# A three-stage attention and feed-forward kernel: order of the first weight loads, place of the later weight conversions, and order of three pools at the join to the last layer

## The chip, the cores and the metric

The kernel runs on one core of one Trainium2 chip. The metric is the time of one execution on the device in microseconds, lower is better. TensorE is called PE in the profile (PEld its weight loads), VectorE DVE, ScalarE ACT, GpSimd POOL, SyncE SP; here SP only issues transfers.

## What is computed

The reference has three parts; each one's output is the next one's input. In the attention, keys and values are first pooled into 32 memory slots per head:

```
a = softmax(phi over the sequence)             # 8 x 8 heads, 576 positions, 32 slots
k_m, v_m = einsum(a, k), einsum(a, v)          # 32 x 64 per head
attn = softmax(q @ k_m.T / 8) @ v_m            # q and k are drawn 200 times larger
x  = attn as (4608, 512)
x1 = (silu(x @ w_gate) * (x @ w_val)) @ w_out  # 512 -> 1536 -> 512, "first layer"
h  = x1 @ w_in                                 # 512 -> 2048, "second layer"
out = where(h > 0, h, exp(min(h, 0)) - 1) @ w2_out   # 2048 -> 512
```

All weights arrive as 64-bit floats. [...]

## The kernel before

**Conversion of a weight tile.** `load_w` (line 87) fetches a 128x512 tile of 64-bit numbers (512 KB) into a buffer of pool `wr` (4 buffers) by a transfer that SP issues (line 89), and then rebuilds it: one ACT instruction (line 101) and four on DVE (lines 102, 103, 105, 106). A gate/value tile (`load_wg`, `split=False`) ends with one more DVE addition (line 113). A tile that is used as a sum of two reduced-precision halves (`load_wo`, `load_w2`) ends with an ACT copy (line 108) and two operations (lines 110, 111), on DVE for the first four output tiles (`own`) and on POOL for all others. Once the first unit has run, line 99 keeps a conversion's instructions behind the last `h` that was computed at the time of its tracing.

**First layer, first pass.** Eight batches of 576 tokens. The value matrix of the attention is folded into the gate and value weights: `vw(b, p)` (line 135) multiplies a batch's pooled values with the tiles `WG[p]`. A unit is then a gate product, a value product, a nonlinearity on ACT and DVE, and a split of the result (`gate1`, `val1`). The first pass runs units 0 to 3 of all batches (weights `WG[0]`, `WG[1]`, output tiles `WO[0]` to `WO[3]`) and, between these units, the attention of the batches to come: `front_tasks(b + 2)` (softmax of phi, pooling of keys and values) and `back_tasks(b + 1)` (scores, their softmax). The list `todo` holds those tasks in the order written; `tick()` takes some of them after every step. The weights `WG[2]`, `WG[3]` and `WO[4]` to `WO[7]`, which only the second pass uses, are converted as items of that list (lines 400 to 409).

**Second pass and third.** The next two passes over the batches (lines 502 to 522) run units 4 to 7 and 8 to 11, adding to partial sums that lie in DRAM; conversions of the remaining weights come from the list `conv`. **Second layer:** nine blocks of 512 tokens with 16 units each (lines 580 to 591): 12 matmuls up, minimum, exponential, tanh, product and maximum on DVE and ACT, a split into two halves, and 12 matmuls down two units later. Ten weight conversions are left over for its first block; `w2q` says from which pool each takes its tiles.

**What sets the order.** The program is written as one stream; a scheduler with a timing model gives each engine its order, with the written order as priority. Each engine works through its own order without overtaking. Pools are taken from two stacks of on-chip memory; a pool that is opened where others were closed overlays their tiles, and its first tiles wait until the old tiles at these addresses are no longer used. At the join to the second layer (lines 526 to 531) the right-hand stack loses `p1` (partial sums), `av` (attention outputs), `t` and `h` (first-layer temporaries and results), and gets `wc` (weights), `h3` (results of a second-layer unit) and `t3` (temporaries of a unit), in this order.

Sizes per partition, from the shapes and buffer counts: `h` 18,432 bytes, then `t` 4,608, `av` 18,432, `p1` 4,608. In their place: `wc` 24,576, `h3` 16,384, `t3` 8,192. So `t3` begins 40,960 bytes in and overlays the end of `av`, all of `p1`, and memory beyond it.

**At the start**, line 361 loads phi and all five key/value tiles of batch 0, then the four gate/value tiles of `WG[0]` and the two query tiles (lines 362 to 367).

Of the kernel before, what the change touches and what calls it, by code (L numbers as in the profile page):

```python
# [27 lines left out]
NCH = 5  # L28
# [9 lines left out]
def attention_moe_moe(ctx: ExitStack, tc: tile.TileContext, qT, phiT, kv, kv4, w1g, w1o, w2, out):  # L38
# [5 lines left out]
    w1g, w1o, w2 = w1g.bitcast(I32), w1o.bitcast(I32), w2.bitcast(I32)  # L44
# [5 lines left out]
    wa_p = ctx.enter_context(tc.tile_pool(name="wa", bufs=NWA))  # L50
# [33 lines left out]
                call()  # L84


    def load_w(store, u, i, src, pool, split=True, own=False):
        raw = wr_p.tile([128, 512, 2], I32, tag="wr", name="wr")
        nc.sync.dma_start(out=raw, in_=src.rearrange("p (n t) -> p n t", t=2))
        lo32, hi32 = raw[:, :, 0], raw[:, :, 1]  # L90
        if split:
            hi = pool.tile([128, 512], F32R, tag="w", name="whi")
            lo = pool.tile([128, 512], F32R, tag="w", name="wlo")
        else:
            full = pool.tile([128, 512], F32, tag="w", name="wg")
        v = wt_p.tile([128, 512], F32, tag="wv", name="wv")
        c = wt_p.tile([128, 512], I32, tag="wc", name="wc")
        vi, cf = v.bitcast(I32), c.bitcast(F32)
        with tc.issue_after(last["h"].ins) if "h" in last else nullcontext():

            act(out=v, in_=hi32.bitcast(F32), func=AF.Copy, scale=2.0 ** -112)
            nc.vector.tensor_scalar(out=c, in0=vi, scalar1=3, scalar2=None, op0=ALU.logical_shift_left)
            stt(out=vi, in0=vi, scalar=-2 ** 31, in1=c, op0=ALU.bitwise_and, op1=ALU.bitwise_or)

            nc.vector.tensor_scalar(out=c, in0=vi, scalar1=-2 ** 23, scalar2=None, op0=ALU.bitwise_and)
            stt(out=cf, in0=lo32.bitcast(U32), scalar=2.0 ** -52, in1=cf, op0=ALU.mult, op1=ALU.mult)
            if split:
                act(out=hi, in_=v, func=AF.Copy)
                part = tt if own else nc.gpsimd.tensor_tensor
                part(out=v, in0=v, in1=hi.bitcast(F32), op=ALU.subtract)  # L110
                part(out=lo, in0=v, in1=cf, op=ALU.add)
            else:
                tt(out=full, in0=v, in1=cf, op=ALU.add)
        store[u][i] = (hi, lo) if split else full


    WG = [[None] * KD for _ in range(NU1 // 2)]
# [1 line left out]
    W2 = [[None] * 2 for _ in range(NU2)]  # L119

    def load_wg(p, k, pool):
        load_w(WG, p, k, w1g[p, k], pool, False)

    def load_wo(u, pool):
        load_w(WO, u, 0, w1o[u], pool, own=u < UA)
# [3 lines left out]


    VW = {}

# [57 lines left out]
    class Batch:  # L192
# [13 lines left out]
        def load_q(self, hf):  # L206
            t = self.qr[hf] = bk_p.tile([128, 4, HS], F32, tag="qr", name="qr", bufs=NQ)
            nc.sync.dma_start(out=t, in_=qT[self.b, hf].rearrange("p (j s) -> p j s", j=4))
# [142 lines left out]
    def load(z):  # L351
        z.load_phi()
        for c in range(NCH):
            z.load_kv(c)
# [3 lines left out]
            z.load_q(c)  # L358


    load(Bs[0])
    Bs[0].phi()
    run(front_tasks(0))
    for k in range(KD):
        load_wg(0, k, wa_p)
    load_q(Bs[0])
    run(back_tasks(0))
    vw(0, 0, G2)
    for k in range(KD):
# [14 lines left out]
    def load2(b):  # L384
        at2[b] = av_p.tile([128, 2, 2, S], F32R, tag="at", name="at2")
        nc.sync.dma_start(out=at2[b].bitcast(F32), in_=at_d[b].bitcast(F32))
# [3 lines left out]
    for b in range(B):  # L390
# [3 lines left out]
        if b == 0:  # L394
            wo = [lambda u=u: load_wo(u, wa_p) for u in range(UA)]
            f1 = [lambda: (Bs[1].phi(), load_q(Bs[1]))] + list(front_tasks(1)) + [lambda: Bs[2].phi()]
            for i in range(max(len(wo), len(f1))):
                todo += wo[i:i + 1] + f1[i:i + 1]
        if 1 <= b <= 4:
            bk += [lambda k=k, p=2 + (b - 1) // 2: load_wg(p, k, wa_p) for k in (0, 1) if b % 2] + \  # L400
                [lambda k=k, p=2 + (b - 1) // 2: load_wg(p, k, wa_p) for k in (2, 3) if b % 2 == 0]
        if b == B - 2:
            wb_p = ctx.enter_context(tc.tile_pool(name="wb", bufs=NWB))
            ps_vw = ctx.enter_context(tc.tile_pool(name="ps_vw", bufs=1, space=PSUM))
            V2 = [(ps_vw, "vw"), (ps_gv, "g")]
            fr += [lambda u=u: load_wo(u, wb_p) for u in (4, 5, 6)]
        if b == B - 1:
            fr.append(lambda: load2(0))
            fr += [lambda: load_wo(7, wb_p), lambda: vw(0, 2, V2), lambda: vw(0, 3, V2)]
        for i in range(max(len(bk), len(fr))):  # L410
            todo += fr[i:i + 1] + bk[i:i + 1]
        if b + 1 < B:
# [112 lines left out]
    pend = []  # L525
    st_p1.close()
    st_r.close()
    wc_p = ctx.enter_context(tc.tile_pool(name="wc", bufs=NWC, side="right"))
    w2q = [wa_p] * 4 + [wc_p] * 6
    h3_p = ctx.enter_context(tc.tile_pool(name="h3", bufs=4, side="right"))  # L530
    t3_p = ctx.enter_context(tc.tile_pool(name="t3", bufs=2, side="right"))


    NC3 = T // 128
# [45 lines left out]
    for j in range(NB):  # L580
        xt, accs = nxt, []
        for u in range(NU2):
            pend.append((j, u, unit3(u, xt), accs))
            if len(pend) > LAG:
                down3(pend.pop(0))
            if w2q:
                more_w2(w2q.pop(0))
            if u == NU2 // 2 and j + 1 < NB:
                nxt = load3(j + 1)
# [38 lines left out]
```

## Time and profile before

| | us |
|---|---|
| three runs: lowest, median, highest | 1585.65, 1587.75, 1588.77 |
| the profiled execution's own time | 1587.06 |
| its span from first to last instruction | 1584.9 |
| PE busy | 1523.7 (96% of the span) |
| DVE busy | 1013.3 (64%) |
| ACT busy | 649.6 (41%) |
| POOL busy | 113.4 (7%) |

A span of the profile is 2.2 us shorter than that execution's own time. "Granted clock" is the share of TensorE's full clock (2.4 GHz) that it was given: 1.00 is full, 0.50 is 1.2 GHz. In an instruction's row, the bracket at the end gives how long the engine stood idle before it and what ended this.

### The profile page before, as it was taken

The numbers are of one execution on the slowest core, as the hardware profiler recorded it, in microseconds if no ns is written. First come the engines' busy times: TensorE is split into PE (matmuls) and PEld (weight loads), VectorE is DVE, ScalarE is ACT, GpSimd is POOL, SyncE is SP. The second block draws the span as 40 slices with busy tenths as digits, with TensorE's granted clock in tenths as the row PEclk, the third lists the DMA queues.
The fourth block names the chain that finished last, engine by engine and source line by source line (L and its number), as shares of the span: only waits on it lengthen the run. The fifth ranks groups of instructions, "written<-read, shape, count | busy, mean of one in ns | idle before, by whom it ended". The sixth has DMA issues, their size and how long they took to land.

```text
span 1584.9 us, 24325 instructions
## 1 busy us (share of the span) xinstructions
PE 1523.7 (96%) x9816; PEld 1307.8 (83%) x9816; DVE 1013.3 (64%) x1798; ACT 649.6 (41%) x1249; POOL 113.4 (7%) x87
## 2 busy tenths in 40 slices
PE   4699999999999999999989999999999999999998
PEld 2567889899999999899967888888888888888887
DVE  7999777635666666667798655555555555555554
ACT  3555544533333333433444434333343434343332
POOL 0000000200011112111343000000000000000000
PEclk7899999999999999999999999999999999999999
DMA  9788422425444455544520101010010101010000
GB/s 361 247 298 310 154 95 73 165 77 190 160 158 167 157 175 180 190 157 154 171 72 9 54 1 54 0 47 8 2 52 1 54 1 53 1 54 0 27 1 27
DMA packets 81008, 164.63 MB, mean 104 GB/s; under 512 B 7168, under 2 KB 54272, under 8 KB 77824
## 3 DMA queue, kind: packets, MB, share of 16 engines
q1 hardware_dynamic: 71680, 153.64, 28.4%
q10 hardware_dynamic: 9216, 9.44, 1.7%
q8 instruction: 77, 1.26, 0.3%
q14 instruction: 35, 0.29, 0.1%
HBM read 115.87 MB, written 47.19 MB: 103 GB/s over the span
## 4 chain that ended last, share of the span: by engine, by line
PE 84%; DVE 11%; DMA 3%; issue 1%; ACT 1%; SPq 0%; ACTq 0%; DVEq 0%
PE acc L567 8%; PE acc L568 8%; PE acc L569 8%; PE pu L543 8%; PE pu L541 8%; PE pu L542 8%; PE acc L158 4%; PE acc L160 4%; PE acc L159 4%; PE pg L153 3%; PE pv L153 3%; PE pg L155 3%; PE pv L155 3%; PE pv L154 3%; PE pg L154 3%; PE pvw L141 3%
## 5 line engine op out<-in xcount | busy, mean ns | idle before, releaser
L541 PE MATMUL pu<-x1s,whi 128*128 128x512 f32 x576 | 225.2, 391 | 4.9 <-DVE g L557 4.9
L567 PE MATMUL acc<-whi,hh 128*128 128x512 f32 x576 | 224.4, 390 | 1.4 <-ACT hh L164 1.4
L543 PE MATMUL pu<-x1s,wlo 128*128 128x512 f32 x576 | 225.1, 391 | 0.0
L542 PE MATMUL pu<-x1s,whi 128*128 128x512 f32 x576 | 225.1, 391 | 0.0
L569 PE MATMUL acc<-whi,hl 128*128 128x512 f32 x576 | 222.5, 390 | 2.6 <-DVE hl L166 2.6
L568 PE MATMUL acc<-wlo,hh 128*128 128x512 f32 x576 | 224.1, 389 | 0.0
L556 DVE SCALAR_TENSOR_TENSOR g<-e,g 128x512 f32<-128x512 f32 x144 | 105.7, 735 | 161.4 <-ACT g L555 161.4
L164 ACT ACTIVATE hh<-g 128x512 fp32r<-128x512 f32 x144 | 91.0, 632 | 216.1 <-DVE g L557 213.1
L554 ACT ACTIVATE e<-g 128x512 f32<-128x512 f32 x144 | 90.7, 631 | 214.9 <-DVE g L553 214.8
L185 DVE SCALAR_TENSOR_TENSOR h<-s,pv 128x288 f32<-128x288 f32 x192 | 86.4, 450 | 110.8 <-PE pv L155 93.5
L166 DVE TENSOR_TENSOR hl<-g,hh 128x512 fp32r<-128x512 f32 x144 | 99.5, 691 | 90.0 <-ACT hh L164 89.9
L158 PE MATMUL acc<-hh,whi 128*128 128x288 f32 x512 | 151.2, 298 | 0.0
L159 PE MATMUL acc<-hh,wlo 128*128 128x288 f32 x512 | 150.0, 294 | 0.0
L160 PE MATMUL acc<-hl,whi 128*128 128x288 f32 x512 | 146.4, 294 | 0.0
L164 ACT ACTIVATE hh<-h 128x288 fp32r<-128x288 f32 x192 | 84.8, 442 | 125.5 <-DVE h L185 124.1
L553 DVE TENSOR_SCALAR g<-pu 128x512 f32<-128x512 f32 x144 | 99.1, 689 | 57.3 <-PE pu L543 53.8
L166 DVE TENSOR_TENSOR hl<-h,hh 128x288 fp32r<-128x288 f32 x192 | 98.1, 511 | 52.3 <-ACT hh L164 52.3
L541 PEld LDWEIGHTS pu<-x1s,whi 128*128 128x128 f32 x576 | 108.6, 189 | 27.8 <-DVE g L557 5.3
L569 PEld LDWEIGHTS acc<-whi,hl 128*128 128x128 f32 x576 | 108.0, 188 | 27.3 <-DVE hl L166 5.0
L567 PEld LDWEIGHTS acc<-whi,hh 128*128 128x128 f32 x576 | 108.3, 188 | 24.2 <-ACT hh L164 1.9
L542 PEld LDWEIGHTS pu<-x1s,whi 128*128 128x128 f32 x576 | 108.8, 189 | 22.4
L543 PEld LDWEIGHTS pu<-x1s,wlo 128*128 128x128 f32 x576 | 108.6, 189 | 22.4
(89 smaller groups left out, 3169.8 us busy)
## 6 DMA issues: line engine op xcount, KB each, us to landing
at<-atd SPq DMA_DIRECT2D x16, 1152.0 KB, 7.0
kvr<-kv SPq DMA_DIRECT2D x32, 512.0 KB, 7.2
wr<-w SPq DMA_DIRECT2D x32, 512.0 KB, 3.8
wr<-w1g SPq DMA_DIRECT2D x24, 512.0 KB, 5.9
qr<-qT SPq DMA_DIRECT2D x16, 576.0 KB, 7.5
atd<-at SPq DMA_DIRECT2D x8, 1152.0 KB, 5.4
p1d<-p ACTq DMA_DIRECT2D x64, 144.0 KB, 1.9
p1l<-p1d SPq DMA_DIRECT2D x16, 576.0 KB, 4.8
```

Of the source, the lines that this page charges most:

```text
L158: mm(ps, lhsT=w[0][:, ms], rhs=hs[0], start=start, stop=False)
L159: mm(ps, lhsT=w[1][:, ms], rhs=hs[0], start=False, stop=False)
L160: mm(ps, lhsT=w[0][:, ms], rhs=hs[1], start=False, stop=stop)
L164: act(out=hh, in_=h, func=AF.Copy)
L166: tt(out=hl, in0=h, in1=hh.bitcast(F32), op=ALU.subtract)
L541: mm(ps, lhsT=wh[:, k, :], rhs=xh, start=k == 0, stop=False)
L542: mm(ps, lhsT=wh[:, k, :], rhs=xl, start=False, stop=False)
L543: mm(ps, lhsT=wl[:, k, :], rhs=xh, start=False, stop=k == KD - 1)
L556: stt(out=g, in0=e, scalar=1.0, in1=g, op0=ALU.add, op1=ALU.mult)
L567: mm(accs[c], lhsT=hs[0][:, cs], rhs=wh, start=u == 0, stop=False)
L568: mm(accs[c], lhsT=hs[0][:, cs], rhs=wl_, start=False, stop=False)
L569: mm(accs[c], lhsT=hs[1][:, cs], rhs=wh, start=False, stop=u == NU2 - 1)
```

## The change

Three edits. (1) At the start, the four tiles of `WG[0]` are fetched by themselves (`fetch_w`), placed among the loads of batch 0: one before the first key/value tile, one after the second, one after the last, one between the two query tiles. Their conversion stays where it was. (2) `WG[2]` is converted in batches 4 and 5 instead of 1 and 2; `WG[3]` in batches 6 and 7 instead of 3 and 4; `WO[4]` to `WO[7]` all in batch 7 (4 to 6 were in batch 6, 7 in batch 7), with the products `vw(0, 2)` and `vw(0, 3)` between and behind them. (3) At the join, the three pools are opened in the order `t3`, `h3`, `wc`; and of the ten conversions left for the second layer, two come in every three units instead of one in each unit.

```
+    def fetch_w(src):
         raw = wr_p.tile([128, 512, 2], I32, tag="wr", name="wr")
         nc.sync.dma_start(out=raw, in_=src.rearrange("p (n t) -> p n t", t=2))
+        return raw
...
-    load(Bs[0])
-    Bs[0].phi()
+    z = Bs[0]
+    z.load_phi()
+    raw[0, 0] = fetch_w(w1g[0, 0])
+    z.load_kv(0)
+    z.load_kv(1)
+    raw[0, 1] = fetch_w(w1g[0, 1])
+    for c in range(2, NCH):
+        z.load_kv(c)
+    raw[0, 2] = fetch_w(w1g[0, 2])
+    z.load_q(0)
+    raw[0, 3] = fetch_w(w1g[0, 3])
+    z.load_q(1)
+    z.phi()
     run(front_tasks(0))
     for k in range(KD):
         load_wg(0, k, wa_p)
-    load_q(Bs[0])
...
-        if 1 <= b <= 4:
-            bk += [lambda k=k, p=2 + (b - 1) // 2: load_wg(p, k, wa_p) for k in (0, 1) if b % 2] + \
-                [lambda k=k, p=2 + (b - 1) // 2: load_wg(p, k, wa_p) for k in (2, 3) if b % 2 == 0]
+        if 4 <= b <= 5:
+            bk += [lambda k=k: load_wg(2, k, wa_p) for k in ((0, 1) if b == 4 else (2, 3))]
         if b == B - 2:
...
-            fr += [lambda u=u: load_wo(u, wb_p) for u in (4, 5, 6)]
+            fr += [lambda k=k: load_wg(3, k, wa_p) for k in (0, 1)]
         if b == B - 1:
+            fr += [lambda k=k: load_wg(3, k, wa_p) for k in (2, 3)]
             fr.append(lambda: load2(0))
-            fr += [lambda: load_wo(7, wb_p), lambda: vw(0, 2, V2), lambda: vw(0, 3, V2)]
+            fr += [lambda u=u: load_wo(u, wb_p) for u in (4, 5)]
+            fr += [lambda: vw(0, 2, V2)]
+            fr += [lambda u=u: load_wo(u, wb_p) for u in (6, 7)]
+            fr += [lambda: vw(0, 3, V2)]
...
+    t3_p = ctx.enter_context(tc.tile_pool(name="t3", bufs=2, side="right"))
+    h3_p = ctx.enter_context(tc.tile_pool(name="h3", bufs=4, side="right"))
     wc_p = ctx.enter_context(tc.tile_pool(name="wc", bufs=NWC, side="right"))
     w2q = [wa_p] * 4 + [wc_p] * 6
-    h3_p = ctx.enter_context(tc.tile_pool(name="h3", bufs=4, side="right"))
-    t3_p = ctx.enter_context(tc.tile_pool(name="t3", bufs=2, side="right"))
...
-            if w2q:
+            if w2q and u % 3 < 2:
                 more_w2(w2q.pop(0))
```

## Rows read from the trace of the kernel before

**Rows 1.** Busy time per stretch of the start; columns named in the first line.

```profile
core 0: us, PE busy (x) PEld busy (x) DVE busy (x) ACT busy (x) POOL busy (x), PEclk, DMA share, GB/s
...
10.00:15.00 5.00, 5.00 (x84) 3.46 (x82) 2.40 (x5) 2.22 (x4) 0.00 (x0) 1.00 1.03 408
15.00:20.00 5.00, 1.38 (x34) 0.39 (x18) 4.97 (x12) 1.78 (x4) 0.00 (x0) 0.84 1.03 420
```

**Rows 2.** Instructions in order of time, first 15 us: start, duration, engine, line, tiles.

```profile
4.75 1.35 DVE L214 TENSOR_REDUCE nmx<-ph 128x2 f32<-128x1152 f32 x1 [4.75 <-DMA ph<-phiT]
...
7.58 0.19 ACT L217 ACTIVATION_READ_ACCUMULATOR ph<-ph,nmx 128x1 f32 x1
...
11.83 0.66 ACT L101 ACTIVATE wv<-wr 128x512 f32<-128x512 f32 x1 [0.68 <-DMA wr<-w1g]
...
12.53 0.43 DVE L102 TENSOR_SCALAR wc<-wv 128x512 int32<-128x512 int32 x1 [4.37 <-ACT wv L101]
...
14.63 0.23 PEld L253 LDWEIGHTS ps_kvm<-kvr,a 64*32 64x32 f32 x16 [0.38 <-issue]
```

**Rows 3.** Groups of DVE instructions by line, 12 to 60 us: busy us, mean ns.

```profile
L103 DVE SCALAR_TENSOR_TENSOR wv<-wv,wc 128x512 int32<-128x512 int32 x12 | 8.1, 684 | 0.1
...
L113 DVE TENSOR_TENSOR wg<-wv,wc 128x512 f32<-128x512 f32 x8 | 5.3, 676 | 0.0
L102 DVE TENSOR_SCALAR wc<-wv 128x512 int32<-128x512 int32 x12 | 5.0, 417 | 4.5 <-ACT wv L101 4.4
```

**Rows 4.** Busy time per stretch as in group 1, about one batch each, batches 1 to 7.

```profile
72.00:117.00 45.00, 42.29 (x557) 30.36 (x557) 41.13 (x88) 24.60 (x57) 0.00 (x0) 1.00 0.83 276
117.00:157.00 40.00, 37.03 (x430) 30.47 (x431) 36.92 (x83) 22.58 (x53) 0.00 (x0) 1.00 0.86 311
157.00:196.00 39.00, 37.27 (x396) 32.19 (x391) 31.95 (x71) 19.85 (x47) 0.00 (x0) 1.00 0.45 164
196.00:231.00 35.00, 32.95 (x276) 28.82 (x275) 28.14 (x61) 16.63 (x37) 0.00 (x0) 1.00 0.28 104
231.00:263.00 32.00, 31.61 (x248) 29.06 (x247) 20.48 (x43) 15.22 (x35) 0.00 (x0) 1.00 0.22 83
263.00:297.00 34.00, 31.01 (x237) 27.60 (x236) 24.49 (x43) 16.56 (x37) 8.60 (x6) 1.00 0.40 134
297.00:331.00 34.00, 33.58 (x267) 31.34 (x266) 15.17 (x31) 16.85 (x38) 3.12 (x2) 1.00 0.27 95
```

**Rows 5.** Who waited longest in total, whole program: us in total, times, longest.

```profile
ACT wv L101 <- POOL wlo L111: 56.0, 31, 3.9
```

**Rows 6.** Instructions in order of time at the join, PE.

```profile
786.36 0.69 PE L160 MATMUL acc<-hl,whi 128*128 128x288 f32 x4
...
792.57 0.39 PE L543 MATMUL pu<-x1s,wlo 128*128 128x512 f32 x1
797.84 0.79 PE L541 MATMUL pu<-x1s,whi 128*128 128x512 f32 x1 [4.88 <-DVE g L557]
```

**Rows 7.** Instructions in order of time at the join, DVE.

```profile
787.89 1.55 DVE L475 TENSOR_TENSOR p1l<-acc,p1l 128x288 f32<-128x288 f32 x4 [1.59 <-DMA p1l<-p2d]
792.89 1.29 DVE L553 TENSOR_SCALAR g<-pu 128x512 f32<-128x512 f32 x2 [3.45 <-DMA x1d<-p1l]
```

**Rows 8.** Busy time per stretch as in group 1, first units of the second layer.

```profile
797.00:857.00 60.00, 55.08 (x223) 43.40 (x224) 58.91 (x80) 27.96 (x46) 30.87 (x20) 0.95 0.16 53
831.00:833.00 2.00, 1.08 (x5) 0.56 (x3) 1.97 (x3) 0.16 (x1) 1.92 (x2) 1.00 0.73 258
```

**Rows 9.** Groups of DVE instructions by line, 797 to 857 us: busy us, mean ns.

```profile
L556 DVE SCALAR_TENSOR_TENSOR g<-e,g 128x512 f32<-128x512 f32 x10 | 13.0, 1302 | 0.6 <-ACT g L555 0.6
L103 DVE SCALAR_TENSOR_TENSOR wv<-wv,wc 128x512 int32<-128x512 int32 x10 | 8.7, 874 | 0.1
L106 DVE SCALAR_TENSOR_TENSOR wc<-wr,wc 128x512 f32<-128x512 uint32 x10 | 8.7, 875 | 0.2
L102 DVE TENSOR_SCALAR wc<-wv 128x512 int32<-128x512 int32 x10 | 7.8, 784 | 0.0
```

**Rows 10.** Two matmuls of the steady second layer, in order of time.

```profile
1002.43 0.39 PE L541 MATMUL pu<-x1s,whi 128*128 128x512 f32 x1
...
1007.87 0.39 PE L541 MATMUL pu<-x1s,whi 128*128 128x512 f32 x1
```

More of the change, by code (lines that the diff above doesn't have):

```diff
@@ L84, in together, with load_w @@
                 call()
-    def load_w(store, u, i, src, pool, split=True, own=False):
+    def fetch_w(src):
         raw = wr_p.tile([128, 512, 2], I32, tag="wr", name="wr")
         nc.sync.dma_start(out=raw, in_=src.rearrange("p (n t) -> p n t", t=2))
+        return raw
+    def load_w(store, u, i, src, pool, split=True, own=False, raw=None):
+        if raw is None:
+            raw = fetch_w(src)
         lo32, hi32 = raw[:, :, 0], raw[:, :, 1]
@@ L121, in load_wg @@
     def load_wg(p, k, pool):
-        load_w(WG, p, k, w1g[p, k], pool, False)
+        load_w(WG, p, k, w1g[p, k], pool, False, raw=raw.pop((p, k), None))
     def load_wo(u, pool):
@@ L131, in attention_moe_moe @@
     VW = {}
+    raw = {}
     def vw(b, p, pools):
```

## The prediction, made before the changed kernel was run

> **What bounds the kernel now.** I read the busy time of each engine by stretch first, then the order of instructions where PE was not full, then the groups of DVE's instructions there. From the second pass on PE is full, and in the steady second layer a unit of 24 matmuls takes 1007.87 - 1002.43 = 5.44 us [rows 10], 0.227 each. The change touches three places where PE is not full. (a) The first 60 us: DVE is free half of 10 to 15 us, works without a pause from 15 us on, and PE waits for it [rows 1]. (b) Batches 1 to 7 of the first pass, where PE is idle for 2.7, 3.0, 1.7, 2.1, 0.4, 3.0 and 0.4 us, the difference between a stretch and PE's busy time in it [rows 4]. (c) The join to the second layer: PE fills its four result buffers, stops at 792.57 + 0.39 = 792.96 and starts again at 797.84 [rows 6], runs at the low granted clock for part of what follows, and then goes no faster than DVE, busy for 58.91 of 60 us [rows 8].
>
> **Edit 1, the first weights among the keys.** A conversion of a gate tile costs DVE two instructions like L103 (0.68), two like L102 (0.42) and L113 (0.68), 2.88 us [rows 3]. Phi has landed at 4.75 [rows 2]; the queue then moves 408 GB/s [rows 1], 1.28 us for 512 KB. The first weight is now sixth behind phi and is picked up by ACT at 11.83; DVE's first conversion step starts at 12.53 [rows 2]. Put first behind phi it lands at about 6.0; ACT is done with phi's exponentials at 7.77 [rows 2], so with 0.66 of ACT DVE starts at about 8.5, 4.0 us earlier. The second weight (behind two key tiles) lands at 4.75 + 4 x 1.28 = 9.9, before the first conversion ends at 11.4; the third (three and a half tiles later) at 14.4, for DVE at 15.0. At 15.0 DVE will have done 5.76 us of conversion instead of 2.47, a lead of 3.3 us, and behind that it is the bound. The keys pay: the last one lands at 4.75 + 6.5 x 1.28 = 13.1, 2.6 us later, but PE begins with it at 14.63 [rows 2], so 1.5 us of cover is left. Without that cover the edit would cost up to 2.6. The lead shrinks wherever DVE then meets a load of batch 1 that lands no earlier, since the queue is full throughout [rows 1]; a fifth weight waits on SP for a buffer, with the loads of batch 1 queued behind it, and that wait ends earlier too. I take -2.5, bounds -4.0 and +2.6.
>
> **Edit 2, conversions moved to the last batches.** Two gate conversions are 5.8 us of DVE. Batches 1, 2 and 3 lose 5.8 each, batch 4 keeps its two, batch 5 gets two, batch 6 changes three output tiles for two gate tiles, batch 7 gets two gate and three output tiles more. Their transfers move with them on SP's queue, which in batches 2 and 3 frees a queue that was busy at 0.86 and 0.45, and in batch 7 has room (0.27) [rows 4]. For PE's idle time I use DVE's share of a stretch as the scale: 0.80 gave 2.1 us (batch 4), 0.64 gave 0.4 (batch 5), and 0.72 with POOL at work gave 3.0 (batch 6) [rows 4]. Batches 1 to 3 come to shares of 0.79, 0.78 and 0.67: about 2.3 + 2.3 + 0.5 = 5.1 instead of 7.4, a gain of 2.3. Batch 5 rises to (20.5 + 5.8)/32 = 0.82, a loss of 1.6. An output tile costs DVE four of these instructions in the stretched form that they have beside POOL: 0.87 + 0.88 + 0.78 [rows 9] and at least 0.42 for the last, about 3.0. Batch 6: (24.5 - 9.0 + 5.8)/34 = 0.63, a gain of 2.6. Batch 7: (15.2 + 9.0 + 5.8)/34 = 0.88, like batch 2 (0.92, 3.0 idle) or a little over for POOL: a loss of 3. Sum: -0.3. What is queued behind a conversion on ACT and DVE is the gate's nonlinearity and the splits, and PE, with three result buffers, waits for these. The scale says nothing of the order that the scheduler will choose; I take -1, bounds -6 (all idle time of batches 1 to 3, less what batch 7 pays at least) and +5.
>
> **Edit 3, the pools at the join.** The first minimum of the second layer needs a `t3` tile. `t3` overlays `p1`, so it waits for the store of the last partial sums: DVE's additions end at 789.44, and the minimum starts at 792.89, 3.45 us later, released by that store [rows 7]. ACT waits beside it. In the new order `t3` and `h3` overlay `h`, `t` and the end of `av`; their last reader is the down product that ends at 787.05 [rows 6], before DVE is through with its additions. So the minimum starts at about 789.4, and PE, which today resumes 4.95 us after it, at about 794.4: idle 1.4 instead of 4.88. `wc` now overlays `p1`, but its first tile is wanted six units later. Late next is DVE: from 797 to 857 us it is full, with ten conversions, while PE's 223 matmuls of that stretch need 223 x 0.227 = 50.6 us [rows 8]. A conversion there costs 3.0 us [rows 9], and with two per three units three fewer fall into the same ten units: 58.9 - 9 = 49.9, just under PE's 50.6. So PE becomes the bound. Today it takes 857 - 792.96 = 64.0 us for these matmuls, a loss of 13.4; afterwards I put the loss at 1.4 of idle time and 1.5 for units in which two conversions follow each other. Gain 10.5. The lower bound is the shift of 3.45 alone, the upper one 13. The slower pace of conversions is hidden as long as unit 14's tile, asked for at unit 9, is there five units (27 us) later; unit 15's has three units, 16 us.
>
> POOL's share in this bears on the sum. L556 takes 1302 ns in this stretch on the mean [rows 9], and DVE is full with POOL at work for half of the time (30.87 of 60) [rows 8]. The Trainium skill ("SBUF — State Buffer", Who interferes with whom) says that DVE and POOL share a pair of ports as an exclusive lock, and that a DVE instruction with two inputs in on-chip memory is blocked fully while POOL reads. By it, ten units would cost DVE their own time plus all of POOL's, so that it would stay the bound with seven conversions, too, and edit 3 would give back only 3.45; that is the second case below. The rows bear it out in part: L556 and the conversions are stretched, but DVE's 58.91 us with 30.87 of POOL's inside leave room for the 20 to 25 us of unstretched work only if POOL blocks it for part of its time.
>
> **Sum.** -2.5 - 1 - 10.5 = -14.0 us. The profiled execution took 1587.06 (span 1584.9 and 2.2 around it), 0.7 under the median of 1587.75. 1587.06 - 14.0 = 1573.1, and from the median 1573.75: I predict 1573.5.
>
> **Rivals.**
> - *DVE beside POOL stays the bound at the join.* The idle time is only moved into later units. For it: DVE's 98% there. Against: three conversions fewer. 3.45 + 3.5 = 7 us: 1580.5.
> - *The reorder does not take the wait away*, because the scheduler puts the last down products behind the first four up products on PE, and the minimum waits for these. PE's first four units of up products end at 792.96 [rows 6], so the minimum starts about when it does now. Only edits 1 and 2 count: 1584.
> - *Short pauses cost the clock.* PE's pauses at the join stay under 1.5 us, but several follow each other. In the rows, PE at 1.08 of 2 us kept a granted clock of 1.00, the 2.4 GHz level [rows 8]. The Trainium skill ("TensorE: Matmul & The Clock Gate", A second HAM failure mode) tells of kernels whose short pauses between groups of matmuls make the clock swing; no row here shows it after so short a pause. As a mechanism of this kernel: today's stretch has a mean clock of 0.95 [rows 8], so 0.05 x 60 x 2 = 6 us at the 1.2 GHz level, which cost 3. If this stays, 1576.5.
> - *Slower: the last batch is overfilled.* ACT, which works in order, waited up to 3.9 us for POOL's end of a conversion [rows 5], with the gate's nonlinearity behind it. Four such waits and two gate conversions of 2.9 on DVE are 21.3 us; 3 are in the sum already. If PE, with three buffers, gets all of it, 1573.5 + 18.3 = 1592. It decides for slower once more than 14 us of it reach PE. Against: batch 6 carries three such tiles beside a whole attention and loses 3.0 in all [rows 4].
>
> **How the numbers follow.** Forecast 0.60; DVE and POOL stay the bound 0.16; the clock 0.09; no effect at the join 0.08; slower 0.05; the rest, 0.02, for less than 0.2% either way. 0.2% (3.2 us) is about what a measurement of this kernel can tell from no change. The forecast's own bounds, with the terms falling independently, are about 1567 to 1579. The range reaches down to 1566 (edits 1 and 2 at two thirds of their bounds) and up to 1582, past the case of a bound DVE, and leaves out the last two. The case at 1584 lies at the edge of faster, and I split it: faster 0.89, same 0.06, slower 0.05.
>
> **What would show it.** Edit 1: DVE's first conversion step at about 8.5 us instead of 12.53, and PE's first gate products some 2.5 us earlier. Edit 2: DVE's share under 0.8 in batches 1 to 3 and near 0.9 in batch 7, with PE's idle time there near 3. Edit 3: the first minimum released by PE's or DVE's own work and not by the store; PE's pause at the join under 2 us; granted clock 1.00 there; DVE no longer full over the next 60 us. The prediction is wrong if the minimum waits as before, or if DVE stays at 98% for ten units.

## The result, and the profile after

The changed kernel takes 1567.49 us (median; 1566.78 to 1568.14), the kernel before, run beside it, 1587.50. The ratio is 0.9874 (95% interval 0.9860 to 0.9889). That is faster, and inside the predicted range, but 6.0 us below the predicted 1573.5. The profiled execution took 1567.55 us with a span of 1565.6, 19.3 less than the 1584.9 before.

Busy time of each engine in the kernel after (the page's first part):

```profile
PE 1518.3 (97%) x9816; PEld 1306.5 (83%) x9816; DVE 1012.6 (65%) x1798; ACT 649.6 (41%) x1249; POOL 112.5 (7%) x87
```

The work is the same. DVE, ACT and POOL are as busy as before within 1 us; what is gone is time in which PE stood still or ran slowly.

**Start.** Instructions in order of time, kernel after (the lines answer to [rows 2]; the conversion that was L101 to L106 is now L106 to L111):

```profile
8.37 0.43 DVE L107 TENSOR_SCALAR wc<-wv 128x512 int32<-128x512 int32 x1 [0.20 <-ACT wv L106]
...
14.45 0.67 ACT L106 ACTIVATE wv<-wr 128x512 f32<-128x512 f32 x1 [1.31 <-DMA wr<-w1g]
15.15 0.43 DVE L107 TENSOR_SCALAR wc<-wv 128x512 int32<-128x512 int32 x1 [0.33 <-ACT wv L106]
```

The first conversion begins on DVE at 8.37 us instead of 12.53. The third one waits for its tile and begins at 15.15, so two are complete by then.

**Batches 1 to 7.** Busy time per stretch, now cut at the first gate product of each batch, so that the same stretch of work can be compared although it lies at other times. First the kernel before, then the kernel after (same columns):

```profile
core 0: us, PE busy (x) PEld busy (x) DVE busy (x) ACT busy (x) POOL busy (x), PEclk, DMA share, GB/s
87.60:134.20 46.60, 42.58 (x495) 34.16 (x493) 41.49 (x92) 24.85 (x57) 0.00 (x0) 1.00 0.85 305
134.20:176.00 41.80, 40.56 (x520) 34.75 (x518) 34.44 (x75) 23.11 (x55) 0.00 (x0) 1.00 0.67 238
176.00:209.00 33.00, 31.27 (x263) 26.92 (x260) 25.72 (x57) 15.30 (x34) 0.00 (x0) 1.00 0.33 118
209.00:241.60 32.60, 30.55 (x257) 26.42 (x257) 26.99 (x59) 15.83 (x34) 0.00 (x0) 1.00 0.29 106
241.60:270.60 29.00, 28.61 (x226) 26.06 (x225) 19.26 (x43) 13.81 (x31) 0.00 (x0) 1.00 0.22 83
270.60:303.80 33.20, 29.79 (x226) 26.14 (x225) 24.24 (x42) 15.76 (x35) 8.60 (x6) 1.00 0.42 140
303.80:338.20 34.40, 34.40 (x275) 32.39 (x274) 11.97 (x25) 15.57 (x34) 3.12 (x2) 1.00 0.37 129
```

```profile
85.30:126.80 41.50, 40.88 (x489) 33.27 (x487) 37.36 (x81) 22.86 (x55) 0.00 (x0) 1.00 0.89 302
126.80:164.80 38.00, 37.81 (x447) 33.59 (x443) 28.40 (x63) 20.57 (x51) 0.00 (x0) 1.00 0.71 246
164.80:198.40 33.60, 33.23 (x343) 28.82 (x341) 22.89 (x51) 15.53 (x36) 0.00 (x0) 1.00 0.24 89
198.40:232.00 33.60, 30.83 (x258) 26.47 (x258) 27.10 (x60) 15.93 (x34) 0.00 (x0) 1.00 0.29 103
232.00:261.90 29.90, 29.04 (x226) 26.09 (x225) 23.94 (x53) 15.15 (x33) 0.00 (x0) 1.00 0.31 115
261.90:292.00 30.10, 28.82 (x227) 26.05 (x226) 19.68 (x42) 13.56 (x31) 0.00 (x0) 1.00 0.40 137
292.00:329.20 37.20, 35.19 (x275) 32.41 (x274) 26.01 (x45) 20.15 (x43) 11.69 (x8) 1.00 0.54 190
```

The first batch line begins at 85.3 instead of 87.6: the start gave 2.3 us. (Over all runs below that add no transfers at the start, this product comes between 84.5 and 85.3 us with the new start and between 87.0 and 88.0 with the old one.) Batches 1 to 3 issue the same number of matmuls (1278 and 1279) in 113.1 us instead of 121.4, 8.3 less; PE's idle time in them falls from 7.0 to 1.2, and its busy time by 2.5. Batches 4 to 7 (984 and 986 matmuls) take 130.8 instead of 129.2, 1.6 more: batch 6 gives back 3.1 and batch 7 takes 2.8. The second pass begins at 329.2 instead of 338.2, 9.0 us earlier.

**Join.** Instructions in order of time, kernel after: DVE, then PE, then a stretch of 60 us with the columns of above (they answer to [rows 7], [rows 6] and [rows 8]):

```profile
779.00 1.55 DVE L494 TENSOR_TENSOR p1l<-acc,p1l 128x288 f32<-128x288 f32 x4 [1.51 <-DMA p1l<-p2d]
780.47 1.28 DVE L574 TENSOR_SCALAR g<-pu 128x512 f32<-128x512 f32 x2
```

```profile
785.31 0.50 PE L562 MATMUL pu<-x1s,whi 128*128 128x512 f32 x1 [1.61 <-DVE g L578]
...
852.86 0.50 PE L564 MATMUL pu<-x1s,wlo 128*128 128x512 f32 x1 [0.73 <-POOL wlo L116]
```

```profile
787.00:847.00 60.00, 60.00 (x263) 48.65 (x263) 53.51 (x77) 30.36 (x49) 24.21 (x16) 1.00 0.16 53
```

The minimum (L574) follows DVE's own additions without a gap; PE pauses for 1.61 us instead of 4.88 and then issues 263 matmuls in 60 us instead of 223, at a granted clock of 1.00 instead of 0.95. One late weight costs 0.73. What all this gave can be read from the last value product of the first layer to the first up product of unit 16, PE in order of time, before and after:

```profile
779.53 0.29 PE L155 MATMUL pv<-at,vw 128*128 128x288 f32 x1
...
877.31 0.39 PE L541 MATMUL pu<-x1s,whi 128*128 128x512 f32 x1
```

```profile
770.27 0.29 PE L161 MATMUL pv<-at,vw 128*128 128x288 f32 x1
...
857.98 0.39 PE L562 MATMUL pu<-x1s,whi 128*128 128x512 f32 x1
```

97.8 us have become 87.7, 10.1 less. So of the 19.3 us, 2.3 come from the start, 6.7 from batches 1 to 7 and 10.1 from the join; 0.2 is left over.

### The profile page after: what moved, and what is told of

Same layout as the page of the kernel before. It is cut to its first block, busy times and chain, and to the rows that moved or that the text cites. A ratio compares the mean times of both kernels' runs of the same rounds, so it can differ in the third digit from the quotient of the medians.

```text
span 1565.6 us, 24339 instructions
## 1 busy us (share of the span) xinstructions
PE 1518.3 (97%) x9816; PEld 1306.5 (83%) x9816; DVE 1012.6 (65%) x1798; ACT 649.6 (41%) x1249; POOL 112.5 (7%) x87
## 4 chain that ended last, share of the span: by engine, by line
PE 79%; DVE 8%; ACT 2%; DMA 1%; issue 1%; POOL 0%; ACTq 0%; DVEq 0%; POOLq 0%
PE acc L589 8%; PE acc L588 8%; PE acc L590 8%; PE pu L564 7%; PE pu L563 7%; PE pu L562 7%; PE acc L164 4%; PE acc L166 4%; PE acc L165 4%; PE pg L159 3%; PE pv L159 3%; PE pv L160 3%; PE pv L161 3%; PE pg L161 2%; PE pg L160 2%; PE pvw L147 2%
## 5 line engine op out<-in xcount | busy, mean ns | idle before, releaser
L574 DVE TENSOR_SCALAR g<-pu 128x512 f32<-128x512 f32 x144 | 99.2, 689 | 51.8 <-PE pu L564 51.6
L562 PEld LDWEIGHTS pu<-x1s,whi 128*128 128x128 f32 x576 | 108.2, 188 | 24.4 <-DVE g L578 2.0
L159 PE MATMUL pg<-at,vw 128*128 128x288 f32 x384 | 118.6, 309 | 9.1 <-ACT at L315 5.7
L589 PEld LDWEIGHTS acc<-wlo,hh 128*128 128x128 f32 x576 | 108.3, 188 | 22.4
```

What stands on the lines that cost most here:

```text
L159: mm(ps, lhsT=wh, rhs=ah, start=g == 0, stop=False)
L562: mm(ps, lhsT=wh[:, k, :], rhs=xh, start=k == 0, stop=False)
L589: mm(accs[c], lhsT=hs[0][:, cs], rhs=wl_, start=False, stop=False)
```

## Experiments

Spans of experiments are compared with the 1584.9 of the kernel before; the medians of that kernel in the runs beside the experiments were 1585.89 to 1587.83. A span is that of one execution, and two executions of the same instructions differ by some us, so the length of the stretch that an edit touches is the better measure.

### One edit at a time

**The start alone** (the kernel before with `fetch_w` and the new order of the first loads):

```
-    load(Bs[0])
-    Bs[0].phi()
+    z = Bs[0]
+    z.load_phi()
+    raw[0, 0] = fetch_w(w1g[0, 0])
+    z.load_kv(0)
...
+    raw[0, 3] = fetch_w(w1g[0, 3])
+    z.load_q(1)
```

> Edit 1 alone (first weight tiles among the keys; everything else as before). Theory: the three edits add up, and the 19.4 us less of span that the changed kernel has are 2.3 by the start, 7 by the moved conversions, 10 at the join. Then this kernel is 2 to 3 us faster than before (about 1585), DVE's first conversion step starts at 8.4 us, and batches 1 to 3 lose PE time as before. Rival: the lead of DVE at the start carries into batches 1 to 3, and part of what these gained in the changed kernel comes from edit 1: then 4 to 7 us faster (1581 to 1583), with batches 1 to 3 shorter than before.

Measured: 1583.20 us against 1587.83, ratio 0.9972 (0.9962 to 0.9983), span 1581.4. Batch 1's first gate product comes at 84.7 instead of 87.6, and the second pass at 336.1 instead of 338.2. Batches 1 to 3 take 46.7, 41.5 and 32.9 us, as long as before (3.4 us of the first lie at the low clock, which is worth at most half of that). The lead goes through them, but does not make them faster.

**The moved conversions alone:**

```
-        if 1 <= b <= 4:
-            bk += [... load_wg(p, k, wa_p) ...]
+        if 4 <= b <= 5:
+            bk += [lambda k=k: load_wg(2, k, wa_p) for k in ((0, 1) if b == 4 else (2, 3))]
...
-            fr += [lambda u=u: load_wo(u, wb_p) for u in (4, 5, 6)]
+            fr += [lambda k=k: load_wg(3, k, wa_p) for k in (0, 1)]
```

(and batch 7 as in the change.)

> Edit 2 alone (gate tiles and output tiles of the second pass converted in the last batches; start and join as before). Theory: 6 to 8 us faster (1580 to 1582), with batches 1 to 3 shorter by about 8 us in sum, batches 4 and 5 longer by 1 each, batch 6 shorter by 3 and batch 7 longer by 3. Rival of the prediction's own scale (DVE's share sets PE's idle time): 0 to 2 us faster (1586), batches 1 to 3 shorter by 2.3 in sum. Second rival: edit 1 made the batches shorter, then 3 us or less here.

Measured: 1579.54 us, ratio 0.9947 (0.9934 to 0.9959), span 1577.5, 7.4 less. Batches 1 to 3 take 41.8, 38.0 and 33.5 us, batches 4 to 7 together 129.9: this edit has the whole gain of the first batches, and the scale by DVE's share, which gave 0 to 2, falls. The sum of these three, in the columns of above:

```profile
sum 113.30, PE 111.89 PEld 95.54 DVE 88.57 ACT 58.99 POOL 0.00; mean PE 37.30 PEld 31.85 DVE 29.52 ACT 19.66 POOL 0.00
```

What PE waited for in batches 1 to 3 (us in total, times, longest) shows where it lay, first in the kernel before, then with this edit:

```profile
PE pvw L141 <- DVE vw L146: 2.0, 4, 0.8
PE ps_aT L237 <- ACT ph L217: 1.7, 1, 1.7
PE pvw L141 <- DVE h L185: 0.9, 1, 0.9
PE ps_kvT L267 <- DVE kvm L260: 0.8, 1, 0.8
...
```

```profile
PE pg L153 <- DVE s L178: 0.6, 1, 0.6
PE pvw L141 <- DVE vw L146: 0.4, 1, 0.4
PE pvw L141 <- ACT p L378: 0.3, 1, 0.3
```

PE's waits add up to 6.8 us before, with the three left out here, and to 1.3 afterwards. Two thirds of those before (4.5 of 6.8) were for the chain of the coming batches: phi's exponentials, the pooled keys and values (`kvm`), the folded weights (`vw`); the others were for the running batch's own results. The 1.7 for phi's exponentials come from the queue: this phi landed at 122.0 us, behind two weight tiles issued ahead of it that landed at 117.5 and 120.4.

**The order of the pools alone:**

```
+    t3_p = ctx.enter_context(tc.tile_pool(name="t3", bufs=2, side="right"))
+    h3_p = ctx.enter_context(tc.tile_pool(name="h3", bufs=4, side="right"))
     wc_p = ...
...
-    h3_p = ...
-    t3_p = ...
```

> Only the order of the three pools at the join (t3, h3, wc); the ten leftover conversions still come one per unit. Theory: the wait for the store goes, PE pauses under 2 us at the join and keeps its clock, but with ten conversions in ten units DVE (58.9 us of work) stays the bound against PE's 50.6, so 4 to 6 us faster (1582 to 1583). Rival: the store's wait and the clock that fell after it were all of it, and the pace matters not: 9 to 10 us faster (1577 to 1578).

Measured: 1580.72 us, ratio 0.9956 (0.9944 to 0.9969), span 1579.6, 5.3 less. The stretch from the last value product to the first up product of unit 16 takes 93.6 us instead of 97.8. DVE at the join, and the 60 us behind it:

```profile
788.80 1.28 DVE L555 TENSOR_SCALAR g<-pu 128x512 f32<-128x512 f32 x2
```

```profile
794.00:854.00 60.00, 55.35 (x233) 42.54 (x232) 58.52 (x80) 29.38 (x48) 30.59 (x20) 1.00 0.15 53
```

The wait for the store is gone and the clock stays at 1.00, but DVE is still full (58.52 of 60), and PE issues 233 matmuls, ten more than in [rows 8]. The prediction's first rival is what happens when only this half of the edit is made.

**The pace of the conversions alone:**

```
-            if w2q:
+            if w2q and u % 3 < 2:
```

> Only the pace of the leftover conversions (two per three units instead of one per unit); pools in the old order. Theory: the minimum still waits 3.4 us for the store, PE pauses about 4.9 us and the clock falls, but DVE has three conversions less in the next 60 us: 3 to 5 us faster (1583 to 1584). Rival: without the new pool order the pace gains nothing, within 1 us of before.

Measured: 1580.71 us, ratio 0.9954 (0.9940 to 0.9967), span 1578.6, 6.3 less: a little more than expected. The stretch at the join takes 91.6 us.

```profile
792.60 1.29 DVE L553 TENSOR_SCALAR g<-pu 128x512 f32<-128x512 f32 x2 [3.44 <-DMA x1d<-p1l]
```

```profile
797.00:857.00 60.00, 59.46 (x251) 49.02 (x252) 52.79 (x77) 29.57 (x49) 25.47 (x16) 0.95 0.15 53
```

Here the store's wait of 3.44 us stands as before, with the low clock behind it (0.95), but DVE has room (52.79 of 60) and PE issues 251 matmuls. Both halves are needed, and they add up: the join becomes 4.2 and 6.2 us shorter by one of them alone, 10.1 by both together.

The four spans alone give 3.5 + 7.4 + 5.3 + 6.3 = 22.5, the whole change 19.3; by the medians it is about 27 against 20. The kernel before enters such a sum four times, and its single executions beside these runs lie between 1584.05 and 1589.88. By the stretches that the edits touch it is 2.1 (begin of the second pass), 7.4 (the same), 4.2 and 6.2 (join), together 19.9; that the edits add up is shown by these stretches and not by the times.

### What the conversions cost in batches 1 to 3

Three accounts were open: DVE's time, the transfers, and the place of the conversions behind the attention in the list.

**The place** (the kernel before, with the gate conversions of batches 1 to 4 at the head of the batch's list instead of its end):

```
-            bk += [... load_wg(p, k, wa_p) ...]
+            bk = [lambda k=k, p=2 + (b - 1) // 2: load_wg(p, k, wa_p) for k in ((0, 1) if b % 2 else (2, 3))] + bk
```

> The kernel before, with the gate conversions of batches 1 to 4 put at the head of the batch's second list (before the scores) instead of at its end, just ahead of the products with the next batch's values; the same batches, the same amount. Theory: it is the place that cost, since the in-order DVE held the copies of these products behind two conversions; then 3 to 5 us faster than before (1583 to 1585), and PE's waits for the copies of pvw in batches 1 to 3 go. Rival: it is the amount of DVE's work in these batches, wherever it stands; then within 1.5 us of before. Second rival: at the head they hold up phi and the scores instead: slower by 2 or more.

Measured: 1593.64 us against 1585.89, ratio 1.0044 (1.0029 to 1.0059): slower. Batches 1 and 2, and what DVE waits for in batches 1 to 3:

```profile
87.40:137.00 49.60, 44.03 (x494) 36.34 (x493) 43.03 (x95) 25.38 (x57) 0.00 (x0) 0.93 0.79 286
137.00:181.20 44.20, 41.51 (x522) 35.22 (x520) 33.25 (x73) 22.78 (x54) 0.00 (x0) 1.00 0.63 224
```

```profile
DVE nmx L214 <- DMA ph<-phiT: 7.8, 3, 3.8
```

Batch 1 takes 49.6 us instead of 46.6, which the low clock alone could explain (6.8 us of it, worth at most 3.4). Batch 2 takes 44.2 instead of 41.8 at the full clock, and DVE waits 7.8 us for phi instead of 4.7. The end of the list was the better place. My reading is that earlier conversions put their transfers ahead of phi and their instructions ahead of what PE waits for; no run takes these two apart.

**The transfers, first attempt** (the moved conversions, plus six transfers into a buffer that nothing reads, two in each of batches 1 to 3):

```
+        if 1 <= b <= 3:
+            bk += [lambda k=k: fetch_only(w1g[3, k]) for k in (0, 1)]
```

> Edit 2 alone, plus two transfers of a weight tile (512 KB each) in each of batches 1, 2 and 3 that nothing reads, at the place where the conversions were; no conversion with them. Theory: the transfers ahead of phi's were a part of the cost (one wait of 1.7 us at 124 us before the change), so 1.5 to 2.5 us slower than edit 2 alone (1581 to 1582). Rival: transfers are hidden, within 0.8 us of edit 2 alone.

Measured: 1588.66 us, ratio 1.0013 (1.0004 to 1.0022), span 1586.0. As a test of batches 1 to 3 it missed: nothing held these transfers back, and all six were issued between 13.1 and 46.0 us. Batch 1's first gate product moved from 87.5 to 93.4, and the second pass from 330.7 to 339.7. What it shows is that the start has no room on the queue: 3 MB there delayed batch 1 by 5.9 us. Of the 9.0 at the second pass, two stretches of 3.4 us at the low clock can explain up to 3.4.

**DVE's time** (the moved conversions, plus two conversions of zeros that lie on the chip, in each of batches 1 to 3; no transfer; each conversion also brings its ACT instruction):

```
-        raw = wr_p.tile(...)
-        nc.sync.dma_start(out=raw, ...)
+        if src is None:
+            raw = raw_d
...
+        if 1 <= b <= 3:
+            bk += [lambda k=k: load_w([[None] * 2], 0, k, None, dm_p, False) for k in (0, 1)]
```

> Edit 2 alone, plus two gate conversions on ACT and DVE (from a tile of zeros on the chip, without a transfer) in each of batches 1, 2 and 3, at the place where the conversions were. Theory: DVE's work at that place was most of the cost, so 4 to 6 us slower than edit 2 alone (1583.5 to 1585.5). Rival, the scale of the prediction (DVE's share of the batch): about 2.3 us slower (1582). Together with the run with transfers alone the two differences should come to the 8 us that batches 1 to 3 gained; if they come to much less, the two work only jointly.

Measured: 1584.76 us, ratio 0.9986 (0.9978 to 0.9995), span 1583.5, 6.0 more than with the moved conversions alone. Batches 1 to 3:

```profile
87.00:130.50 43.50, 42.33 (x493) 34.07 (x491) 41.39 (x92) 24.52 (x57) 0.00 (x0) 1.00 0.86 301
130.50:172.50 42.00, 40.96 (x521) 34.88 (x519) 34.68 (x75) 23.30 (x55) 0.00 (x0) 1.00 0.60 212
172.50:208.40 35.90, 34.18 (x261) 29.04 (x259) 25.69 (x56) 15.46 (x34) 0.00 (x0) 0.90 0.22 79
```

They take 121.4 us, 8.1 more than the 113.3 without these instructions; 1.6 came back at the join, where this execution was at the low clock for 3.4 us and the other for 6.8. In the third batch PE ran at the low clock for 6.9 us, which is worth at most 3.4; so this work costs 4.7 to 8.1 us here, and not the 2.3 of the scale.

**The transfers, held** (the moved conversions, plus two unread pairs of transfers that SP may issue only right before the load of phi for one of the batches ahead):

```
+            if self.b in (5, 7):
+                with tc.issue_after(last["sp"].ins):
+                    for k in (0, 1):
+                        t = dm_p.tile([128, 512, 2], I32, tag="dm", name="dm")
+                        nc.sync.dma_start(out=t, in_=w1g[3, k]...)
```

> Edit 2 alone, plus two pairs of weight-tile transfers (512 KB each) that nothing reads, each pair on SP's queue directly ahead of a phi load of a batch in the middle of the first pass, as two pairs stood before the change; held there by an order behind the query loads before them. (The run with transfers alone sent them out in the first 50 us, so this place is untried.) Theory: a pair makes phi land some 2.6 us later, DVE and then PE wait for a part of it, so 1.5 to 4 us slower than edit 2 alone (1581 to 1583). Rival: it is DVE's work alone that counted, transfers are hidden: within 1 us of edit 2 alone.

Measured: 1582.23 us against 1587.38, ratio 0.9971 (0.9961 to 0.9981), span 1580.1, 2.6 more than without. The pairs landed at 98.4 and 99.7 us and at 141.9 and 143.1, ahead of phi at 101.4 and 145.0. In the kernel before there were two such pairs, too, each one load of phi later. Batches 1 and 2:

```profile
87.10:130.20 43.10, 41.50 (x473) 33.53 (x471) 35.96 (x77) 22.58 (x54) 0.00 (x0) 0.96 0.83 300
130.20:169.90 39.70, 39.05 (x463) 32.94 (x455) 29.89 (x65) 20.40 (x51) 0.00 (x0) 1.00 0.78 276
```

They take 43.1 and 39.7 us instead of 41.8 and 38.0, 3.0 more. In batch 1, 3.4 us at the low clock (mean 0.96) can explain 1.7 of them; batch 2 is at the full clock, and the six other runs with the moved conversions and nothing added take 37.9 to 38.2 us for it. So transfers ahead of phi cost 1.3 to 3.0 us in these batches, the instructions 4.7 to 8.1. Both causes are shown to cost, the instructions more. With the low clock taken off, the two come to 6.0 us. What they have to explain is itself known to 1.6 us only: batches 1 to 3 of the kernel before take 121.4 us in its own profile and 119.8 in that of the run with the pools alone, which has the same first pass.

### Batch 7: DVE's share or POOL

**The last two steps of `WO[4]` to `WO[7]` on DVE** (the kernel after):

```
-        load_w(WO, u, 0, w1o[u], pool, own=u < UA)
+        load_w(WO, u, 0, w1o[u], pool, own=u < 2 * UA)
```

> The changed kernel, with the last two steps of the conversions of WO[4] to WO[7] on DVE instead of POOL, so that POOL is idle in batch 7. Theory: batch 7's loss of about 3 us comes from DVE's full queue, so moving 5.4 us more onto DVE makes it 1 to 3 us slower (1568.5 to 1570.5). Rival: it comes from POOL, through DVE's stretched instructions and ACT's waits; then 1 to 2 us faster (1565.5 to 1566.5).

Measured: 1564.59 us (1563.84 to 1566.47), ratio 0.9868 (0.9853 to 0.9882), span 1562.2. The time alone does not tell it from the changed kernel: the two ratios' intervals overlap. Batch 7 in this kernel, then groups of DVE's instructions in batch 7 (busy us, mean ns) in the kernel after and in this one:

```profile
291.10:326.30 35.20, 34.88 (x274) 32.41 (x273) 25.66 (x53) 20.56 (x43) 0.00 (x0) 1.00 0.58 202
```

```profile
L108 DVE SCALAR_TENSOR_TENSOR wv<-wv,wc 128x512 int32<-128x512 int32 x6 | 5.5, 932 | 0.0
L172 DVE TENSOR_TENSOR hl<-h,hh 128x288 fp32r<-128x288 f32 x9 | 5.3, 589 | 1.5 <-ACT hh L170 1.5
```

```profile
L172 DVE TENSOR_TENSOR hl<-h,hh 128x288 fp32r<-128x288 f32 x9 | 4.1, 454 | 1.0 <-ACT hh L170 1.0
L108 DVE SCALAR_TENSOR_TENSOR wv<-wv,wc 128x512 int32<-128x512 int32 x6 | 4.0, 685 | 0.0
```

DVE does eight more instructions (53, not 45) and is busy for less time: 25.66 us, not 26.01, because its others are no longer stretched (932 ns to 685, 589 to 454). PE's idle time in the batch falls from 2.0 us to 0.3, and the batch from 37.2 to 35.2. This is no chance of one execution: batch 7 takes 37.2 us in all six runs that have the moved conversions with POOL's steps, and 35.2 in this run and the next. Of the 2.8 us that it lost, 2.0 were POOL's doing, not that of DVE's share.

PE's longest wait in batch 7 of the changed kernel shows how POOL reached it:

```profile
311.88 1.67 DVE L108 SCALAR_TENSOR_TENSOR wv<-wv,wc 128x512 int32<-128x512 int32 x1
...
313.58 0.63 ACT L113 ACTIVATE whi<-wv 128x512 fp32r<-128x512 f32 x1 [2.02 <-DVE wv L108]
...
314.56 1.09 PE L147 MATMUL pvw<-wg,vt 64*32 64x512 f32 x16 [1.06 <-ACT s L180]
```

A DVE step that takes 0.68 us elsewhere took 1.67 beside POOL. ACT waited 2.02 us for it, the gate's nonlinearity (L180) stood behind that wait on ACT, and PE waited 1.06 for the nonlinearity. ACT also waited 2.7 us directly for POOL's last step of three conversions; how much of the 2.0 that made is not shown.

**No conversion on POOL at all** (`own=True` for all output tiles and all weights of the second layer as well):

```
-        load_w(WO, u, 0, w1o[u], pool, own=u < UA)
+        load_w(WO, u, 0, w1o[u], pool, own=True)
...
-        load_w(W2, u, i, w2[u, :, i * 1024:(i + 1) * 1024], pool)
+        load_w(W2, u, i, w2[u, :, i * 1024:(i + 1) * 1024], pool, own=True)
```

> The changed kernel with the last two conversion steps on DVE for all tiles, POOL doing none, so in batch 7 (as in the run before) and also in the first block of the second layer. Theory: beside POOL a conversion costs DVE about 0.9 us in its own instructions and 0.6 in L556, more than the 1.36 of two further steps, and POOL's 3.1 us of delay to a weight go too; so batch 7 loses 1 us instead of 3 and the join stays at or under 3.6: 2 to 4 us faster than the changed kernel (1563.5 to 1565.5). Rival: DVE, with 1.36 us more in each conversion, becomes the bound at the join; then batch 7's 2 us are given back there, 1566 to 1569.

Measured: 1566.24 us (1563.82 to 1566.99), ratio 0.9866 (0.9850 to 0.9882), span 1562.0. Batch 7 takes 35.2 us again, and no late weight stops PE in the second layer; its pause at the join is 2.3 us instead of 1.6. The median lies outside the 1563.5 to 1565.5 that were expected and at the rival's 1566, but the rival's mechanism is not there: batch 7 keeps its 2 us, and nothing is given back at the join. Against the kernel before that is as good as the last kernel; that it adds something to it is not shown.

### A version that beats both, and the change once more

**No POOL, and the conversions spread by what the batches have room for:** none in batch 4, two in batch 5, three in each of batches 6 and 7; the leftover conversions in every unit from unit 9 on, where no two fall on a DVE still behind.

```
-        if 4 <= b <= 5:
+        if b == 5:
...
+            fr += [lambda p=p, k=k: load_wg(p, k, wa_p) for p, k in ((2, 2), (2, 3), (3, 0))]
...
+            fr += [lambda k=k: load_wg(3, k, wa_p) for k in (1, 2, 3)]
...
-            if w2q and u % 3 < 2:
+            if w2q and (u % 3 < 2 or u > 8):
```

> As the run with all conversion steps on DVE, with no gate conversion in batch 4, two in batch 5, three in batches 6 and 7, and the leftover conversions of the second layer coming once per unit from unit 9 on instead of two in three. Theory: batch 4 no longer loses its 1 us, and the last weight is no longer late (0.9 us at unit 15 in the changed kernel): 1 to 2 us faster than with the steps on DVE alone (1562 to 1564). Rival: three gate conversions beside the last attention cost batches 6 and 7 more than batch 4 gains: equal or up to 2 us slower.

Measured: 1561.41 us (1560.54 to 1562.29), ratio 0.9838 (0.9823 to 0.9854), a little better than expected and better than the change. Batch 4 takes 30.7 us instead of 33.6, batch 6 30.2, as in the changed kernel, and batch 7, with three gate tiles instead of two, 34.5. The 60 us behind the join:

```profile
787.00:847.00 60.00, 60.00 (x267) 49.67 (x265) 57.24 (x102) 32.66 (x55) 0.00 (x0) 1.00 0.15 53
```

DVE now has all the work (57.24 of 60), and PE issues 267 matmuls where it had 263.

**The changed kernel again**, beside the last two:

> The changed kernel once more, on the same chip as the two variants of it in this set, so that they can be compared in one sitting. Both theories: 1566 to 1569, ratio to before near 0.987; a second profile shows how much of batch 7's 3 us of lost PE time and of the join's 3.6 returns from one execution to the next (theory: within 1 us).

Measured: 1567.49 us (1566.88 to 1569.64), ratio 0.9881 (0.9863 to 0.9900), span 1565.0. Up to the join its gate products begin within 0.2 us of those of the first profile. PE's pause at the join is 0.96 us this time, not 1.61. The change's gain and its distribution repeat, and the interval of the spread version does not touch this one's.

## Why the prediction came out as it did

**What bounds the kernel: right.** The three places named are where the time came from, and nothing came from elsewhere (2.3 + 6.7 + 10.1 of 19.3).

**Edit 1: right in size and mechanism.** DVE's first conversion at 8.5 was forecast, 8.37 came; the third tile for DVE at 15.0, 15.15 came; a gain of 2.5, 2.3 came at batch 1. The sign that was named for it was a little off: the first gate product of all is only 1.4 us earlier (31.43 instead of 32.83), the rest is there by batch 1. The keys' cover held: PE begins with the last key tile at 14.64 us, as before (14.63).

**Edit 2: the term that was mis-sized.** It was set at -1; alone it gave 7.4, in the whole change 6.7. This is most of the 6 us that the prediction missed. The parts:

| | forecast | measured (length of the batch) |
|---|---|---|
| batches 1 to 3 | -2.3 | -8.3 |
| batch 4 | 0 | +1.0 |
| batch 5 | +1.6 | +0.9 |
| batch 6 | -2.6 | -3.1 |
| batch 7 | +3.0 | +2.8 |

The step that failed is "For PE's idle time I use DVE's share of a stretch as the scale". The scale said that DVE at 0.79 must cost 2.3 us in a batch, and the sign named for it was a share under 0.8. In the kernel after DVE is busy for 0.90 of batch 1, and PE is idle for 0.6; in batch 4 it is busy for 0.81 and PE is idle for 2.8. What counts in batches 1 to 3 is, for the larger part, whether DVE's queue is late for the chain of the next batches (`kvm`, `vw`): two conversions of 2.9 us in order ahead of it make it late, as the run with conversions of zeros showed (4.7 to 8.1 us). The prediction named the transfers that move along, and gave them no price of their own; ahead of phi they cost 1.3 to 3.0 us. Its lower bound of -6 ("all idle time of batches 1 to 3, less what batch 7 pays at least") was passed in the whole change (6.7) and by the edit alone (7.4), because PE's busy time in these batches fell too (by 2.5), which idle time does not count; why it fell is not shown. The time stayed in the range, 1.5 us above its lower end, only because the other two terms came within 0.4 us of their forecasts.

**Batch 7's loss: right number by luck, wrong reason.** The loss of 3 was put down mostly to DVE at 0.88 of the batch. DVE came to 0.70, in part because the row read for this batch (297 to 331, 15.17 us of DVE) begins 7 us ahead of it (303.8 to 338.2, 11.97 us). With POOL's steps moved to DVE the loss went from 2.8 to 0.8 at the same share and a little more (0.73).

**Edit 3: right.** Gain 10.5 forecast, 10.1 measured; pause 1.4 forecast, 1.61; clock 1.00; DVE at 53.51 of 60 and no longer the bound. Alone, the order gave 4.2 and the pace 6.2, as the sum had put it (the wait 3.45 with its clock; the three conversions). One cover failed: unit 14's and 15's tiles were said to come in time, and one weight was late by 0.73 (row at 852.86). Two readings were off without changing the sum. The new pools reach the beginning of `av` (bytes 23,040 to 24,576), not its end. And the "20 to 25 us of unstretched work" of DVE beside POOL are about 50: 40 instructions of the units at 0.69 us and ten conversions at 2.2. So of POOL's 30.87 us in that stretch about 9 were added to DVE's time.

**The rivals.** DVE beside POOL did not stay the bound, but it does if the pace is left alone (DVE at 58.52 of 60, the run with the pools alone). The reorder did take the wait away. No low clock followed at the join: with the pause at 1.61 the granted clock stayed at 1.00. All eight runs with the old order of the pools pause for 4.1 to 5.1 us there and have 3.4 or 6.8 us at 1.2 GHz at this place; the six with the new order pause for 1.0 to 2.3 us and have none. The last batch was not overfilled: PE lost 2.0 us of idle time there, not 14.

**The Trainium skill's rule on the shared ports** ("SBUF — State Buffer", Who interferes with whom) says that whichever of the two issues first holds the ports and the other waits; so POOL's time need not all fall on DVE, as the prediction took it. Here about half of it did. In batch 7 POOL was busy for 11.69 us; with it away the 45 instructions that DVE has in common take 25.66 less 8 x 0.683, 20.2 us instead of 26.0. So 5.8 us of DVE's time, half of POOL's, were waiting. "Perfetto Trace Analysis" (Optimizing Scalar/DVE Operations) of the Trainium skill says that moving work between these two may not help because they share a port; here moving it back to DVE made batch 7 shorter by 2.0 us.

## What to carry to other kernels

An engine's share of a stretch is no scale for what its work costs another engine: ask which chain is queued behind the instruction, in order, and price a moved step by the waits for that chain (here the table of what PE waited for named it: 5.5 of its 6.8 us went, of 8.1 us gained), with its transfer as a second price wherever the queue is busy. When a new stage overlays old memory, give the first tiles it needs the memory whose last reader is done first, and see whether an engine that works behind it still is full, since either one alone gave half of the gain. Work that was handed to a second engine to relieve the first is worth a try back: with the ports shared it cost DVE 5.8 us to be spared 5.5.

## What the runs showed of the hardware

**The low clock comes and goes in the first pass.** In these two rows (columns as above, first the kernel before, then the run with conversions of zeros) PE has a similar pause, and only the second is followed by the low level, 1.2 GHz, for 6.9 us:

```profile
102.00:105.00 3.00, 1.28 (x10) 0.30 (x10) 3.00 (x8) 2.39 (x7) 0.00 (x0) 1.00 1.00 377
```

```profile
186.00:189.80 3.80, 2.22 (x18) 0.98 (x14) 3.80 (x9) 1.62 (x3) 0.00 (x0) 1.00 0.07 25
189.80:193.20 3.40, 3.27 (x14) 1.60 (x15) 3.25 (x7) 2.38 (x5) 0.00 (x0) 0.50 0.02 5
```

Such a stretch of 3.4 us also lies in the profile of the run with the new pace alone, which does the same work as the kernel before up to there and has none in its own. So one profiled execution can differ from another by 1.7 us (half of 3.4) in the first pass for the same instructions; why it falls in one and not in the other stays open.
